# Attention and two MoE layers on one core: the head and the first pass put under the planner's due times, blocks 0 and 1 in feature halves, PSUM banks from one pool

## The chip, the core and the metric

One NeuronCore of a Trainium2 chip runs the whole program. The metric is the device time of one execution in microseconds (us); before the change the median of three runs is 935.18 us. Engines are named as in the profile: PE (TensorE matmul), PEld (its weight loads), DVE (VectorE), ACT (ScalarE), POOL (GpSimd), SP (the queue that issues nearly all DMAs). TensorE's clock has two levels, 1.2 and 2.4 GHz, and a granted clock of 1.00 is the upper one.

## The reference

Batch 4, 8 heads, 576 positions, head dimension 64; then two feed-forward layers over 2304 tokens, 512 wide, with 2048 features.

```python
# for every head: attention over q, k, v averaged in groups of 4, repeated 4 times,
# plus attention in a band |i - j| < 4; the two results are added
out_up    = np.repeat(sm_attn(mean4(q), mean4(k), mean4(v)), 4, axis=2)
out_local = softmax(where(band, scale * q @ k.T, -1e9)) @ v
x  = (out_up + out_local)                   # as 2304 x 512
h  = x @ w_in;   x = (h * sigmoid(h)) @ w_out                    # layer 1
h  = x @ w_in2;  y = where(h > 0, h, exp(min(h, 0)) - 1) @ w_out2  # layer 2
```

Everything is fp32. The layers' products are made from high and low parts (hi, and lo = x - hi, both fp32r), three matmuls for one product. The weights' 16 tensors of the first pass and all later ones are decoded from pairs of 32-bit words by ACT and DVE before they are split.

## The kernel before, in words

**Three parts.** The *head* is the attention of batch 0 (4 pairs of heads). The *first pass* is the first half of layer 1's features (8 of 16 feature tiles, f = 0 to 7) for 9 blocks of 256 tokens, with the attention of batches 1 to 3 (12 pairs) run between its matmuls. The *paired part* (`paired`, L847) is all the rest: three passes of three "duos" of 768 tokens each, layer 1's second half and both halves of layer 2.

**Attention of a pair** (`attention`, L278) is a generator that stops at every `yield`: transposes of q and k (L293), copies out of PSUM on ACT (L301, L303), pooling by 4 on DVE (L306), banded scores (L315), mask and maximum on DVE, subtraction and scaling on POOL (L330, L389), exponentials on ACT, transposes of the results (L409, L418), and the two products (L426, L438), joined into `x32` on DVE (L446). Rows arrive by `load_rows` and `load_windows` (L199, L237).

**A unit (n, f) of the first pass** is `g1` (L485: 12 matmuls of 128x256 into `ph`, then tanh on ACT, a product on DVE, `gh` on ACT, `gl` on POOL) and, LAG = 3 units later, `g2` (L527: 12 matmuls into two banks y0, y1, evicted after f = 7 and stored). `split_x` (L457) makes a block's hi on ACT (L468) and lo on DVE (L474).

**Weights of the first pass** pass through `decode_w` and `split_w` (L160, L174): two ACT operations, three on DVE, one more on ACT, one on POOL (L182); 16 tensors of 512 KB, loaded into a ring of three (`load_w`, L136).

**What sets the order in the head and the first pass** is written out by hand. The loads stand in a list (L1059 to L1070), and `attention(3)` issues the rows of the next pair (batch 1) in its middle (L345). `step` (L1127) takes turns among the live pairs; `small_first` (L1101) takes turns among weights, paced by EARLY_PACE and DECODE_PACE; `tick` (L1190), called after every third matmul, gives attention a step when a pace counted from deadlines says so. `warm` (L252) puts in matmuls on zeros at fixed places, 40 in all. PSUM is cut into four pools of two banks (L89 to L92): attention takes turns through fixed lists of them (`bank`, L263), `ph` has two banks, a decoding weight two.

**What sets the order in the paired part** is a planner: every operation of ACT, DVE and POOL is a `Job` (L575) with an engine, a cost, predecessors, and a due time. `pump` (L619) puts out those that can start by the planner's clock, earliest start first. Matmuls stand in program order there (L944, L1033, L1035), and `need` forces what they wait for.

Instructions of one engine run in the order in which the program put them out; the planner works when the program is built and not on the chip.

Of the kernel before, what the change touches and what calls it, by code (L numbers as in the profile page):

```python
# [22 lines left out]
def attention_moe_moe2_kernel(ctx, tc, q, k, v, wi1, wo1, wi2, wo2, out):  # L23
# [28 lines left out]
    STEPS = 19  # L52
    TICKS = 8
    DECODE_PACE = 1.5
    EARLY_PACE = 1.2
    N_EARLY = 13
    WARM, FILL = 9, (8, 4, 4, 4)
    GROUP = 3
# [14 lines left out]
    for i in range(NW):  # L73
        lo, hi = a0[i], a0[i + 1] - 1
        assert q0[i] <= lo and hi < q0[i] + WIN
        assert w0[i] <= max(lo - 3, 0) and min(hi + 3, S - 1) < w0[i] + WIN

# [10 lines left out]
    nat = attn_pools.enter_context(tc.tile_pool(name="nat", bufs=2, side="right"))  # L88
    att = attn_pools.enter_context(tc.tile_pool(name="att", bufs=2, side="right"))  # L89
# [6 lines left out]
    mask = cpool.tile([P, NW // 2, WIN], F32, name="mask")  # L96

    def constants():
        make_identity(nc, ident)
        tmp = gp.tile([P, NB], F32, tag="t", name="masktmp")[:, :4 * WIN].rearrange("p (n w) -> p n w", w=WIN)  # L100
# [13 lines left out]


# [3 lines left out]
    wf = {}  # L119
    wt = {}  # L120
    wz = []


# [4 lines left out]
    at = {"unit": 0, "load": 0, "decode": 0, "split": 0, "ahead": 2, "loads": 2 * FP}  # L128

    def load_next():  # L130

        if at["load"] < at["loads"]:
            load_w(at["load"])
            at["load"] += 1

    def load_w(i):  # L136
        layer, f, which = order[i]
        src = wsrc[layer][which].bitcast(I32)
        st = stage.tile([P, 2 * DM], I32, tag="ws", name="ws", bufs=3)
        if which == 0:  # L140
            nc.sync.dma_start(
                st.rearrange("p (c f) -> p c f", c=KC),
                src[:, f * 2 * P:(f + 1) * 2 * P].rearrange("(c p) f -> p c f", p=P),
            )
        else:
            nc.sync.dma_start(st, src[f * P:(f + 1) * P, :])
        wst[i] = st


    def magnitude(i):  # L150

        if i < len(order) and i not in wf:
            st = wst[i].rearrange("p (n w) -> p n w", w=2)
            t = ps_d.tile([P, DM], F32, tag="d", name="pw").bitcast(I32)
            nc.scalar.activation(t.bitcast(F32), st[:, :, 1].bitcast(F32), AF.Abs, scale=65536.0)

            nc.scalar.activation(st[:, :, 0].bitcast(U32), st[:, :, 0].bitcast(U32), AF.Copy, scale=2.0 ** -29, bias=2.0 ** -10 - 0.5)
            wf[i] = t

    def decode_w(i):  # L160
        magnitude(i)
        yield
        st = wst.pop(i).rearrange("p (n w) -> p n w", w=2)
        t = wf[i]
        tf = t.bitcast(F32)
        nc.vector.tensor_scalar(tf, tf, 2.0, W_MAX, op0=ALU.max, op1=ALU.min)
        nc.vector.scalar_tensor_tensor(t, t, 3, st[:, :, 0], op0=ALU.logical_shift_left, op1=ALU.bitwise_or)
        yield
        wf[i] = stage.tile([P, DM], I32, tag="wf", name="wf", bufs=3)
        nc.vector.scalar_tensor_tensor(wf[i], st[:, :, 1], -(1 << 31), t, op0=ALU.bitwise_and, op1=ALU.bitwise_or)  # L170
        load_next()
        yield

    def split_w(i, engine):  # L174
        layer, f, which = order[i]
        src = wf.pop(i).bitcast(F32)
        hi = wpool.tile([P, DM], F32R, tag=f"wh{which}", name=f"wh{which}")
        lo = wpool.tile([P, DM], F32R, tag=f"wl{which}", name=f"wl{which}")
        wt[layer, f, which] = tuple(x.rearrange("p (c f) -> p c f", c=KC) if which == 0 else x for x in (hi, lo))
        nc.scalar.copy(hi, src)  # L180
        yield
        engine.tensor_tensor(lo, src, hi.bitcast(F32), ALU.subtract)  # L182
        yield


    x32 = xpool.tile([P, KC, NT], F32, name="x32")

    pairs = [(b, pr) for b in range(B) for pr in range(NPAIR)]
    loaded = {}
# [3 lines left out]
    borrowed = {}  # L193

    def borrow(i, name):
        at, n = {"qk": (S, 2 * S), "qkD": (3 * S, 2 * SD), "vd": (3 * S + 2 * SD, 2 * SD)}[name]
        return x32[:, pairs[i][1], at:at + n][:, :2 * 2 * D if name == "vd" else n]

    def load_rows(i, which, engine=None):  # L199
        b, h0 = pairs[i][0], 2 * pairs[i][1]  # L200
        src = (q, k, v)[which]
        if which == 2:

            if i < NPAIR:
                heads = [wpool.tile([P, DM], F32R, tag=tag, name="rows2").bitcast(F32) for tag in ("wh0", "wl0")]
            else:
                t = nat.tile([P, 4 * FAC * D], F32, tag="natv", name="rows2", bufs=1)
                heads = [t[:, :DM], t[:, DM:]]
            for j, t in enumerate(heads):
                (engine or nc.sync).dma_start(t[:HS], src[b, h0 + j].rearrange("(p r) d -> p (r d)", r=2 * FAC))  # L210
            loaded[i, which] = heads
            return

        if i in (1, 2):
            both = xs.tile([P, 2 * NB], F32R, tag=("xh", "xl")[which], name=f"rows{which}").bitcast(F32)
            ts = [both[:, :NB], both[:, NB:]]
            half = NTB // 2
            for j in range(2):
                for a in range(2):
                    (engine or nc.sync).dma_start(  # L220
                        ts[a][:TB, :half * 2 * D].rearrange("p (c e) -> p c e", c=half)[:, :, j * D:(j + 1) * D],
                        src[b, h0 + j].rearrange("(c p) d -> p c d", p=TB)[:, a * half:(a + 1) * half],
                    )
                borrowed[2 * i - 2 + which, j] = ts[j]
            loaded[i, which] = [t[:, c * 2 * D:(c + 1) * 2 * D] for t in ts for c in range(half)]
            return
        elif i == 3 and which == 0:
            borrowed["y"] = yp.tile([P, KC * NB], F32, tag="y", name="rows0")
            t = borrowed["y"]
        else:  # L230
            t = nat.tile([P, NTB * 2 * D], F32, tag="nat", name=f"rows{which}", bufs=2)
        t = t[:, :NTB * 2 * D].rearrange("p (c e) -> p c e", c=NTB)
        for j in range(2):
            (engine or nc.sync).dma_start(t[:TB, :, j * D:(j + 1) * D], src[b, h0 + j].rearrange("(c p) d -> p c d", p=TB))
        loaded[i, which] = [t[:, c] for c in range(NTB)]

    def load_windows(i):  # L237
        b, h0 = pairs[i][0], 2 * pairs[i][1]
        if i in (2, 3):
            vw = borrowed["y"][:, (i - 2) * NW * D:(i - 1) * NW * D].rearrange("p (n d) -> p n d", d=D)  # L240
        else:
            vw = nat.tile([P, NW, D], F32, tag="vw", name="vw")
        for j in range(2):
            rows = v[b, h0 + j]
            nc.sync.dma_start(
                vw[j * WIN:(j + 1) * WIN, :NW - 1, :],
                bass.AP(tensor=rows.tensor, offset=rows.offset, ap=[[D, WIN], [w0[1] * D, NW - 1], [1, D]]),
            )
            nc.sync.dma_start(vw[j * WIN:(j + 1) * WIN, NW - 1, :], rows[w0[-1]:w0[-1] + WIN, :])
        loaded[i, 3] = vw  # L250

    def warm(n):  # L252
        pz = ps_h.tile([P, 512], F32, tag="h", name="pz")
        for _ in range(n):
            nc.tensor.matmul(pz, wz[0][:, :P], wz[0][:, :512], start=True, stop=True)

    def load_pair(i):
        for which in range(3):
            load_rows(i, which)

    banks = [(ps_a, "a")]

    def bank(name):  # L263
        pool, tag = banks[0]
        banks.append(banks.pop(0))
        return pool.tile([P, 512], F32, tag=tag, name=name)

    ybanks = [(ps_y, "y0"), (ps_y, "y1")]

    def ybank(name):  # L270
        pool, tag = ybanks[0]
        ybanks.append(ybanks.pop(0))
        return pool.tile([P, 512], F32, tag=tag, name=name)

    def ring(name, n):
        return att.tile([P, NW * WIN], F32, tag="ring", name=name, bufs=5)[:, :n]

    def attention(i):  # L278
        b, pr = pairs[i]

        if i < NPAIR:
# [64 lines left out]
        if i >= 2:  # L346
            load_windows(i)
# [964 lines left out]
```

## Time and profile before

| | us |
|---|---|
| median of 3 runs (lowest, highest) | 935.18 (933.81, 935.58) |
| the profiled execution: its own time | 935.57 |
| its span, from the first to the last instruction | 933.8 |
| PE busy in it | 897.7 (96%) |
| DVE, ACT, POOL busy | 627.2, 537.1, 263.2 |
| DMA traffic | 101.27 MB, 108 GB/s over the span |

The span is 1.8 us shorter than the profiled execution's own time. Busy PE is not PE at its peak, since matmuls are pipelined and overlap in the trace: how fast they go is read from the distance of their starts. The slices of the page are 23.3 us wide.

### The profile page before, as it was taken

To read this page: it belongs to the slowest core of one execution; us is meant where nothing else is said; L and a number is where in the kernel's file an instruction comes from. 1 tells how busy PE (TensorE), PEld (TensorE's weight loads), DVE (VectorE), ACT (ScalarE), POOL (GpSimd) and SP (SyncE) were. 2 spreads that over 40 slices of the span, in tenths; PEclk is the share of its full clock that TensorE was granted. 3 is DMA by queue.
4 is the path that set the end of the run, shared out by engine and by line. 5 is a ranking of instruction groups with operands and counts; after the bars stand their busy time and mean duration, and the time that the engine had idled before them with its cause. 6 is when DMAs were issued, how large, how long until landed. Compare 5 with 4: busy or idle time off the path is not lost.

```text
span 933.8 us, 17299 instructions
## 1 busy us (share of the span) xinstructions
PE 897.7 (96%) x6656; PEld 830.8 (89%) x6661; DVE 627.2 (67%) x1132; ACT 537.1 (58%) x1247; POOL 263.2 (28%) x292
## 2 busy tenths in 40 slices
PE   8388999999999999999999999999999999999998
PEld 5267889998999898999999999889899898998996
DVE  6777554454445758895885987948849979375462
ACT  5676645544545556844825748648458586382550
POOL 3676554454452223231101322301013023000000
PEclk9679999999999999999999999999999999999999
DMA  9954443332339402623533225132321350230301
GB/s 186 204 174 106 98 101 80 95 82 65 92 105 316 158 24 80 214 68 125 170 126 95 74 102 170 54 105 91 114 83 52 136 180 35 68 102 34 102 1 68
DMA packets 106531, 101.27 MB, mean 108 GB/s; under 512 B 62544, under 2 KB 89168, under 8 KB 106448
## 3 DMA queue, kind: packets, MB, share of 16 engines
q1 hardware_dynamic: 104048, 99.57, 35.7%
q10 hardware_dynamic: 2400, 0.59, 0.4%
q8 instruction: 52, 0.85, 0.4%
q14 instruction: 31, 0.25, 0.1%
HBM read 76.55 MB, written 23.59 MB: 107 GB/s over the span
## 4 chain that ended last, share of the span: by engine, by line
PE 63%; DVE 2%; ACT 1%; issue 0%; ACTq 0%; DVEq 0%
PE pc L944 28%; PE pc L1035 21%; PE pc L1033 11%; PE y L542 2%; PE ph L498 1%; DVE t L516 0%; DVE raw L713 0%; DVE raw L767 0%; DVE part L997 0%; DVE raw L766 0%; DVE xlr L736 0%; DVE s1t L761 0%; DVE raw L717 0%; ACT t L513 0%; DVE wAA3l L736 0%
## 5 line engine op out<-in xcount | busy, mean ns | idle before, releaser
L522 POOL TENSOR_TENSOR gl<-t,gh 128x256 fp32r<-128x256 f32 x72 | 56.2, 782 | 130.2 <-ACT gh L519 122.1
L542 PE MATMUL y<-gh,wh 128*128 128x256 f32 x288 | 86.9, 302 | 0.0
L498 PE MATMUL ph<-xh,wh 128*128 128x256 f32 x288 | 77.9, 295 | 6.2 <-DVE t L516 5.1
L542 PE MATMUL y<-gh,wl 128*128 128x256 f32 x288 | 82.1, 285 | 0.0
L542 PE MATMUL y<-gl,wh 128*128 128x256 f32 x288 | 82.1, 285 | 0.0
L498 PE MATMUL ph<-xl,wh 128*128 128x256 f32 x288 | 76.2, 289 | 2.9 <-DVE xl L474 2.8
L516 DVE SCALAR_TENSOR_TENSOR t<-t,ph 128x256 f32<-128x256 f32 x72 | 30.0, 416 | 68.0 <-ACT t L513 67.9
L1035 PE MATMUL pc<-wl,grw 128*128 128x512 f32 x192 | 74.8, 389 | 0.0
L1035 PE MATMUL pc<-wh,glk 128*128 128x512 f32 x192 | 74.8, 389 | 0.0
L1035 PE MATMUL pc<-wh,ghk 128*128 128x512 f32 x192 | 74.7, 389 | 0.0
L1035 PE MATMUL pc<-wh,grw 128*128 128x512 f32 x192 | 74.7, 389 | 0.0
L944 PE MATMUL pc<-xhr,wSA 128*128 128x384 f32 x288 | 74.5, 334 | 0.0
L956 ACT COPY hg<-pc 128x384 f32<-128x384 f32 x54 | 25.9, 479 | 65.2 <-PE pc L944 64.3
L498 PEld LDWEIGHTS ph<-xh,wh 128*128 128x128 f32 x288 | 55.2, 192 | 8.6 <-DVE t L516 6.3
L498 PEld LDWEIGHTS ph<-xl,wh 128*128 128x128 f32 x288 | 55.2, 192 | 4.4 <-DVE xl L474 3.7
L542 PEld LDWEIGHTS y<-gh,wh 128*128 128x128 f32 x288 | 56.0, 194 | 2.2 <-issue 1.0
L519 ACT CAST gh<-t 128x256 fp32r<-128x256 f32 x72 | 29.3, 407 | 49.4 <-DVE t L516 49.3
L997 DVE SCALAR_TENSOR_TENSOR part<-pc,part 128x384 f32<-128x384 f32 (+1 forms) x42 | 24.8, 609 | 48.0 <-PE pc L1035 28.4
L542 PEld LDWEIGHTS y<-gl,wh 128*128 128x128 f32 x288 | 56.0, 194 | 0.0
L542 PEld LDWEIGHTS y<-gh,wl 128*128 128x128 f32 x288 | 55.8, 194 | 0.0
L513 ACT ACTIVATE t<-ph 128x256 f32<-128x256 f32 x72 | 27.4, 381 | 48.7 <-PE ph L498 42.6
L736 DVE TENSOR_TENSOR xlr<-xraw,xhr 128x768 fp32r<-128x768 f32 x47 | 46.3, 985 | 13.0 <-ACT xhr L733 12.9
(248 smaller groups left out, 2836.5 us busy)
## 6 DMA issues: line engine op xcount, KB each, us to landing
ws<-in_moe_w_in_dram SPq DMA_DIRECT2D x32, 512.0 KB
ws<-in_moe_w_out_dram SPq DMA_DIRECT2D x32, 512.0 KB
xraw<-x SPq DMA_DIRECT2D x24, 384.0 KB
rows<-in_v_dram SPq DMA_DIRECT2D x36, 144.0 KB
yp<-yo SPq DMA_DIRECT2D x9, 512.0 KB
xd<-x SPq DMA_DIRECT2D x4, 1152.0 KB
x<-part SPq DMA_DIRECT2D x6, 768.0 KB
yp<-yo SPq DMA_DIRECT2D x6, 768.0 KB
```

Source lines behind the costliest of these rows:

```text
L498: nc.tensor.matmul(ph[:, :nb], a[:, c, :], b[c], start=m == 0, stop=m == 3 * KC - 1)
L513: nc.scalar.activation(t, h, AF.Tanh, scale=0.5)
L516: nc.vector.scalar_tensor_tensor(t, t, 1.0, h, op0=ALU.add, op1=ALU.mult)
L519: nc.scalar.copy(gh, t)
L522: nc.gpsimd.tensor_tensor(gl, t, gh.bitcast(F32), ALU.subtract)
L542: nc.tensor.matmul(y[d // 2][:, h:h + nb], wm[:, sl], gm, start=f == 0 and m == 0 and d % 2 == 0, stop=f == FP - 1 and m == 2, skip_group_ ...
L736: other=("V", VEC_[width], lambda: nc.vector.tensor_tensor(lo(), src, hi().bitcast(F32), ALU.subtract)),
L944: nc.tensor.matmul(acc_, a[:, cs], b[:, c, :], start=fresh and c == 0 and m == 0, stop=c == 1 and m == 2, skip_group_check=True,)
L956: snap[after, j] = [Job("A", ACT_[NB], lambda dst=dst, acc_=acc_: nc.scalar.copy(dst, acc_), [], gate, due=soon)]
L997: nc.vector.scalar_tensor_tensor(dst, src, sc, dst, op0=ALU.mult, op1=ALU.add)
L1033: nc.tensor.matmul(y[d][:, :NB], wm[:, sl], gm, start=first, stop=last_)
L1035: nc.tensor.matmul(y[d], gm[:, sl], wm, start=first, stop=last_)
```

## The change

The planner is extended to the head and the first pass. PE and SP become engines of it ("P", "S"), loads are jobs with a modelled DMA time, and every transpose group, score group, g1 and g2 is a job with a due time. `pick` takes the job with the earliest start and, among those of its engine that start within 0.1 us, the one due first. So the generators, paces and hand-written lists go.

- `Slots` and `Hold`: a tile or bank is taken when the job that first writes it is put out, and comes free when its last user is. All eight PSUM banks are one such pool; a rule limits `ph` to 3, `ph` and y together to 6, and weight temporaries to 2. Only the first eight weights use a bank as temporary.
- Blocks 0 and 1 run as (0, f 0 to 3), (1, f 0 to 3), (0, f 4 to 7), (1, f 4 to 7), so that both blocks' y banks (four) are held at once; the other blocks are as before.
- Some operations choose their engine: copies out of PSUM ACT or DVE, attention's subtraction and scaling and pooled values POOL or DVE, x's lo POOL or DVE (it was DVE's), with a preference added (PREFER).
- In the head, until the first g1, `fill` puts a matmul on zeros (128x512) for every 0.22 us of a gap over 0.3 us that the planner sees on PE.
- Rows of batch 0 load whole (before, pairs 1 and 2 in halves); batch 1's loads take their place by due time. `keep_x` stores a batch of x by due time and not after all attention. The constant column for the sums is set three times in all and not once a pair.
- Units of block 0 with f < 3 are split in 8 and 4 matmuls, so that they can start before the weight's low part is there.
- In the paired part a weight's load is modelled by a DMA clock (1.9 + 1.75 + 1.0 us on an idle queue) where it was 7.1 us after the slot came free, the two ACT operations of a decode are two jobs, and the bank sets are those that come free first.

The number of matmuls on data is unchanged.

```diff
-    ps_y = ctx.enter_context(tc.tile_pool(name="ps_y", bufs=1, space=PSUM))
-    ps_h = ctx.enter_context(tc.tile_pool(name="ps_h", bufs=2, space=PSUM))
-    ps_a = ctx.enter_context(tc.tile_pool(name="ps_a", bufs=2, space=PSUM))
-    ps_d = ctx.enter_context(tc.tile_pool(name="ps_d", bufs=2, space=PSUM))
+    psum = ctx.enter_context(tc.tile_pool(name="psum", bufs=1, space=PSUM))
+    PREFER = {("G", "V"): 1.5, ("V", "G"): -1.5, ("A", "V"): 0.5, ("V", "A"): -0.5}
+    LATE, FRAC = 2.0, (0.5, 0.7, 0.85, 1.0)
+    SLACK, MOST_H, N_PSUM, SPLIT_F = 0.1, 3, 8, 3
+    T_MM, T_FIRST, T_PAIR = 0.1185, 44.0, 6.4
...
+    def bank_rule(held, kinds):
...
+        return h.get("h", 0) <= MOST_H and h.get("h", 0) + h.get("y", 0) <= 6 and h.get("w", 0) <= 2
...
+    def fill(t):
+        gap = t - clock_of["P"]
+        if banks.free:
+            filler(min(int((gap - 0.1) / 0.22), 40))
...
+            pj = Job(
+                "P", 0.085 * len(parts), flip, [lq] if n_ == 0 else [lk] if n_ == 1 else [lq, lk], lat=0.2,
...
+        psl = Job("P", 1.25, scores, copies, lat=0.2, takes=bank2 + [hE], uses=[hqk])
...
+        psd = Job("P", 0.5, pooled_scores, [red], lat=0.2, takes=bankd + [hED, hsm], uses=[hqkD])
...
+            pj = Job("P", 0.11 * (s1 - s0), flip, [norm], lat=0.2, takes=[bank] + ([haT] if s0 == 0 else []), uses=[hE])
...
+            pj = Job("P", 0.26, flip, [norm_d], lat=0.2, takes=[bank] + ([haD] if j == 0 else []), uses=[hED])
...
+        psu = Job("P", 0.5, out_d, flips_d + pv, lat=0.2, takes=[banku], uses=[hvd, haD])
...
+            pj = Job("P", 0.54, out_l, [lw] + flips[:1 + t], lat=0.2, takes=[bank], uses=[hw, haT])
...
+        for n in range(0, 2, 2):
+            for f0 in range(0, FP, FP // 2):
+                sequence += [(m, f) for m in (n, n + 1) for f in range(f0, f0 + FP // 2)]
+        sequence += [(n, f) for n in range(2, len(BLOCKS)) for f in range(FP)]
+        at_, t_ = {}, T_FIRST
...
+            t_ += 24 * T_MM + share.get(n, 0.0) * (1.0 if n > 1 else LATE if f >= FP // 2 else 2.0 - LATE)
...
+        run(g1_jobs[0, 0])
+        filling[0] = False
+        run([j for b_ in range(B) for j in batch_end[b_]] + [kept_x[b_] for b_ in range(B)] + [x for p_ in w_split.values() for x in p_])
```

## Rows read from the trace of the kernel before

**Rows 1.** The page, parts 1 and 2: busy time, and the granted clock in 40 slices.

```profile
PE 897.7 (96%) x6656; PEld 830.8 (89%) x6661; DVE 627.2 (67%) x1132; ACT 537.1 (58%) x1247; POOL 263.2 (28%) x292
...
PEclk9679999999999999999999999999999999999999
```

**Rows 2.** Five stretches: length, busy us (x instructions) by engine, clock, DMA share, GB/s.

```profile
0.00:63.40 63.40, 45.98 (x525) 30.59 (x530) 44.66 (x90) 41.58 (x112) 37.68 (x56) 0.78 0.85 191
63.40:84.00 20.60, 14.02 (x134) 12.54 (x132) 17.64 (x30) 14.27 (x31) 11.71 (x11) 0.92 0.47 131
84.00:147.70 63.70, 60.36 (x752) 54.41 (x747) 31.86 (x69) 35.03 (x118) 34.52 (x44) 0.97 0.40 96
147.70:375.00 227.30, 222.38 (x2324) 212.55 (x2323) 126.61 (x250) 117.50 (x329) 91.48 (x112) 0.99 0.37 110
375.00:930.70 555.70, 554.97 (x2934) 520.69 (x2932) 406.42 (x697) 328.74 (x661) 87.78 (x69) 1.00 0.30 98
```

**Rows 3.** The chain that ended last: start us, us, what.

```profile
322.99 1.44 PE y L542 x12
...
367.53 1.04 PE pc L944 x6
...
374.95 26.00 PE pc L944 x150
...
897.28 31.34 PE pc L1035 x138
```

**Rows 4.** PE's instructions in order of time: start us, us, what [idle before].

```profile
5.59 1.03 PE L293 MATMUL pst<-ident,rows 96*128 96x96 f32 x5 [0.25 <-DMA rows<-in_q_dram]
...
19.75 1.67 PE L255 MATMUL pz<-zeros 128*128 128x512 bf16 x7
...
63.37 0.38 PE L498 MATMUL ph<-xh,wh 128*128 128x256 f32 x1
...
78.52 0.86 PE L293 MATMUL pst<-ident,rows 96*128 96x96 f32 x5 [2.04 <-DVE wf L170]
...
80.45 0.41 PE L498 MATMUL ph<-xl,wh 128*128 128x256 f32 x1
80.67 0.41 PE L498 MATMUL ph<-xh,wh 128*128 128x256 f32 x1
...
150.77 0.28 PE L498 MATMUL ph<-xh,wh 128*128 128x256 f32 x1
```

**Rows 5.** 160 to 280 us as in rows 2; then PE's L498 alone; then L542 alone.

```profile
160.00:280.00 120.00, 119.08 (x1418) 111.70 (x1418) 55.25 (x120) 60.83 (x192) 56.45 (x72) 1.00 0.34 88
160.00:280.00 120.00, 48.33 (x334) 42.40 (x332) 1.00 0.34 88
160.00:280.00 120.00, 47.59 (x327) 41.76 (x327) 1.00 0.34 88
```

**Rows 6.** SP's queue in the head: start us, us, line, what it issues.

```profile
1.73 6.47 SPq L220 DMA_DIRECT2D rows<-in_q_dram  x8
...
34.52 0.34 SPq L146 DMA_DIRECT2D ws<-in_moe_w_out_dram  x1
34.91 1.26 SPq L234 DMA_DIRECT2D rows<-in_q_dram  x2
36.69 2.22 SPq L234 DMA_DIRECT2D rows<-in_k_dram  x2
38.95 2.83 SPq L210 DMA_DIRECT2D rows<-in_v_dram  x2
...
44.58 0.53 SPq L141 DMA_DIRECT2D ws<-in_moe_w_in_dram  x1
```

**Rows 7.** Two stretches of the head, columns as in rows 2.

```profile
24.00:48.00 24.00, 10.14 (x91) 6.97 (x94) 17.83 (x34) 16.03 (x45) 15.45 (x19) 0.65 1.00 216
48.00:63.40 15.40, 14.96 (x176) 10.88 (x175) 11.63 (x23) 13.62 (x30) 12.40 (x14) 0.67 0.50 164
```

**Rows 8.** DVE's line L474, its durations: ns shortest/median/longest, first and last start us.

```profile
L474 DVE TENSOR_TENSOR xl<-x,xh x36: 409/426/1348, 57.9 to 339.8; 128x256 fp32r<-128x256 f32 x36
```

More of the change, by code (lines that the diff above doesn't have):

```diff
@@ L186, in attention_moe_moe2_kernel @@
[L186 to L235, printed above, removed]
@@ L252, in warm @@
[L252 to L273, printed above, removed]
@@ new lines, in attention_moe_moe2_kernel, with __init__, can, give @@
+    filling = [True]
+    serial = [0]
+    class Slots:
+        def __init__(self, tiles, rule=None, takes=None, heirs=None):
+            self.free = [(0.0, n, t) for n, t in enumerate(tiles)]
+            self.rule, self.takes, self.heirs = rule, takes, heirs
+            self.held = {}
+            self.busy = {}
+        def can(self, kinds):
+            n = len(kinds)
+            if n > len(self.free) or self.rule is not None and not self.rule(self.held, kinds):
+                return None
+            return sorted(x[0] for x in self.free)[n - 1]
+        def give(self, entry):
+            if self.takes == 0:
+                self.heirs[entry[1]](entry)
+            else:
+                self.free.append(entry)
@@ new lines, in attention_moe_moe2_kernel, with __init__, take, done @@
+    class Hold:
+        def __init__(self, slots, kind=None):
+            self.slots, self.kind, self.tile, self.left, self.last, self.users = slots, kind, None, 0, 0.0, []
+        def take(self):
+            s_ = self.slots
+            self.slot = min(s_.free, key=lambda x: x[:2])
+            s_.free.remove(self.slot)
+            self.tile = self.slot[2]
+            s_.held[self.kind] = s_.held.get(self.kind, 0) + 1
+            s_.busy[self.slot[1]] = self
+            if s_.takes:
+                s_.takes -= 1
+                if s_.takes == 0:
+                    rest, s_.free = s_.free, []
+                    for entry in rest:
+                        s_.give(entry)
+        def done(self, job):
+            self.left -= 1
+            self.last = max(self.last, job.end)
+            if self.left == 0:
+                self.slots.held[self.kind] -= 1
+                del self.slots.busy[self.slot[1]]
+                self.slots.give((self.last, self.slot[1], self.tile))
@@ L583, in sooner, with after @@
+        def after(self, preds):
+            for p in preds:
+                self.preds.append(p)
+                if p.end is None:
+                    if not self.open_:
+                        cand.remove(self)
+                        blocked.add(self)
+                    self.open_ += 1
+                    p.after_me.append(self)
+                    p.sooner(self.due - self.dur - p.lat)
         def sooner(self, due):
@@ L611, in emit @@
             assert t is not None
-            waiting.remove(self)
+            cand.remove(self)
+            for h in self.takes:
+                h.take()
+            if self.eng == "P":
+                if filling[0]:
+                    fill(t)
+                now[0] = t + self.dur
             self.fn()
@@ L636, in need @@
                 need(job.preds)
+                while job.end is None and job.start() is None:
+                    pick().emit()
                 if job.end is None:
@@ new lines, in attention_moe_moe2_kernel, with filler @@
+    banks = Slots(bank_tiles, bank_rule)
+    def filler(n):
+        if n > 0:
+            entry = min(banks.free, key=lambda x: x[:2])
+            for _ in range(n):
+                nc.tensor.matmul(entry[2], wz[0][:, :P], wz[0][:, :512], start=True, stop=True)
+    def fill(t):
+        gap = t - clock_of["P"]
+        if banks.free:
+            filler(min(int((gap - 0.1) / 0.22), 40))
+    wz = []
+    wsrc = [(wi1, wo1), (wi2, wo2)]
+    wst = {}
+    wt = {}
+    GORD = [2 * j for j in range(FP // 2)] + [2 * j + 1 for j in range(FP // 2)]
@@ new lines, in attention_moe_moe2_kernel @@
+        weights_second(0, end_first, lambda k: "w2")
+        x_work(0, end_first, lambda k: "wide" if k < 1 else "ring" if k < 2 else "rest" if k == 2 else (0, k - 3, FP // 2 - 1))
+        last = len(BLOCKS) - 1
+        run([x_split[last, c] for c in range(KC)])
+        x_pools.close()
+        open_wide()
+        xring.append(ring_slot())
+        events["wide"] = now[0]
+        run([j for f in range(FP) for j in g1_jobs[last - 1, f]])
+        xring.append(ring_slot())
+        events["ring"] = now[0]
@@ new lines, in attention_moe_moe2_kernel @@
+        run([j for f in range(FP) for j in g1_jobs[last, f]])
+        open_rest()
+        events["rest"] = now[0]
+        base[0] = now[0] + 12 * T_MM
+        entries = [(a_, n_, t_, []) for a_, n_, t_ in banks.free] + [(1e6 + n_, n_, h_.tile, h_.users) for n_, h_ in banks.busy.items()]
+        entries.sort(key=lambda x: (any(h_ is banks.busy.get(x[1]) for h_ in acc[last]), x[0]))
+        half = len(entries) // 2
+        banksets.extend([[x[2] for x in entries[:half]], [x[2] for x in entries[half:]]])
@@ new lines, in attention_moe_moe2_kernel @@
+        ph1 = paired({e: [x[3] for x in entries[e * half:(e + 1) * half]] for e in range(2)})
+        rest = [j for f in range(FP) for j in g2_jobs[last, f] if j.end is None]
+        while rest:
+            next(ph1)
+            clock_of["P"] = now[0]
+            while rest and rest[0].open_ == 0 and (rest[0].end is not None or (rest[0].start() or 1e9) <= now[0] + 0.1):
+                if rest[0].end is None:
+                    rest[0].emit()
+                rest.pop(0)
+                pump(now[0])
```

1215 lines of the change are left out of this document (617 added, 598 removed).

## The prediction

> **What bounds the kernel now.** I read the page's busy time and clock first, then the busy time by stretches, then the chain that ended last, and PE's and SP's instructions in order of time where the first two show a loss. PE is busy for 96% of the span, and its granted clock is clearly down only in slices 2 and 3 [rows 1]. The stretches divide the kernel in two [rows 2]. From 375 us to the end PE is busy for 554.97 of 555.70 us, and the chain is matmul upon matmul there, from 374.95 us to the last step at 897.28 [rows 3]. Nothing that reorders other engines can shorten this; it can only break it. So everything that can be won lies before 375 us.
>
> The first g1 starts at 63.37 us [rows 4]. From there to 374.95 are 311.6 us. PE's work in them: a group of 12 matmuls takes 1.44 us back to back [rows 3], and 72 units have two groups each, 144 x 1.44 = 207.4 us. For attention I take 160 to 280 us, where PE is busy for 119.08 us and the clock is 1.00: 334 + 327 = 661 matmuls belong to units (x 0.12 = 79.3 us), the other 757 take 39.8 us, and a pair has 121 of them, so a pair costs PE 6.36 us [rows 5]; 12 pairs are 76.3 us. Three groups of the paired part at 1.04 us are mixed into the end [rows 3]: 3.1 us. Together 286.8 us, so 311.6 - 286.8 = 24.8 us are lost. Of that PE is idle for 6.58 + 3.34 + 4.92 = 14.8 us (length less busy time in stretches two to four [rows 2]); the rest is the lower clock and changes between kinds of matmul.
>
> The head is the other loss: 63.4 us for four pairs, which cost PE 4 x 6.36 = 25.4 us at full clock. What limits it? DMA at first: share 1.00 and 216 GB/s from 24 to 48 us [rows 7]. Batch 0's rows are 4 x (6 x 144 + 320) KB = 4.85 MB (shapes of the reference, windows with their overlap), 22.5 us at that rate, but the weights and, from 34.91 to 41.8 us, the rows of batch 1 go in between: no weight load is issued between 34.52 and 44.58 [rows 6]. Of ACT, DVE and POOL none is full: in those 24 us they are busy for 16.03 + 17.83 + 15.45 = 49.3 us, 2.05 engines of three; the densest stretch, 48 to 63.4, has 37.65 / 15.4 = 2.44 [rows 7]. The order costs the rest.
>
> **The change part by part.**
>
> *Head.* By 63.4 us the three engines have done 44.66 + 41.58 + 37.68 = 123.9 us of work [rows 2], with 13 weights begun. The first g1 needs one, and four are needed within the next few units. A weight costs the three engines 5.3 us by the planner's own costs (0.62 + 0.66 + 0.62, 0.70 + 0.69 + 0.69, 1.30), so nine that wait are 47.5 us: 76.4 us remain. Data come at 5.59 us [rows 4]. At 2.05 engines busy that is 5.6 + 37.3 = 42.9 us, at 2.44 it is 36.9. *Fill* adds to it: the planner prices a pair's PE work at 1.02 + 1.25 + 0.5 + 0.55 + 0.52 + 0.5 + 1.08 = 5.42 us where the rows give 6.36, and packs every gap that it sees with matmuls of 0.22 us, which is what they take (seven in 1.67 us [rows 4]). So PE has no slack to catch up: 4 x 0.94 = 3.8 us late. Sum: 46.7 us; I take **48 us** for the first g1. Ends: 41 (denser) and 60 (weights still go first). Fewer, whole loads take six DMAs of 6.47 / 8 = 0.81 us off SP's queue, and batch 1's rows, 1.26 + 2.22 + 2.83 us of issue [rows 6], go behind the weights; both lie inside these 48 us. Next to be late are batch 1's rows; their attention is due only after the first units.
>
> *First pass.* The 286.8 us of PE work stay. Feature halves ask for four features' weights in the first eight units, so the PE idle of the second stretch (6.58 us [rows 2]; 2.04 of it in one wait at 78.52 behind a weight's DVE work [rows 4]) should go in part, but more work now runs in less time. By 147.7 us the engines have done 94.2 (DVE), 90.9 (ACT) and 83.9 (POOL), 269 us in all [rows 2]; block 2 follows at 150.77 [rows 4]. For PE alone block 2 could start at 48 + 29 x 1.44 + 25.4 = 115 us (16 g1, 13 g2, four pairs). At 2.44 engines the other work takes until 5.6 + 110.2 = 116 us, at 2.05 until 137. So PE and the others bind nearly together. **Lost: 15 us** (ends 5 and 30), about what the old order loses after 84 us (24.8 less the second stretch's idle and its clock of 0.92), with some 9 of it before block 2, which then starts near 124.
>
> *PSUM.* While blocks 0 and 1 hold four y banks, ph takes up to two, and attention and weight temporaries share the rest; before, attention had four banks to take turns in. No row prices this wait: nothing at best, and the delay of the third rival at worst; I put it inside the 15.
>
> *x's lo* leaves DVE for POOL in most cases: 36 instructions of 0.43 us off DVE [rows 8], 0.74 on POOL by the planner's cost, beside matmuls; at nothing, since POOL is busy for 91 of 227 us in the fourth stretch [rows 2]. The same instruction has taken 1348 ns against a median of 426 [rows 8]. The Trainium skill's page "SBUF — State Buffer" (section "Who interferes with whom") says that a VectorE instruction with two SBUF inputs and a GpSimd instruction that reads SBUF exclude each other for a whole instruction. The spread in that row agrees; by the rule, what moves to POOL still blocks DVE now and then, by up to the 0.9 us of the row, and the sum would be a few us more where DVE is on the path.
>
> *Paired part.* Same matmuls, same order; 555.7 us stay. Its cover is DVE at 406 of 556 us and ACT at 329 [rows 2]. The shorter modelled load lets ACT queue for a load earlier than it lands; tanh and evictions stand behind it. At nothing, with 0 and +8 as ends: PE can't gain, and a us or so at each of a few stage changes is what idle engine time would not cover. The constant column and the stores of x lie beside other work.
>
> *Sum.* 48 + 286.8 + 15 = 349.8 us instead of 374.95, so 25.2 us less. The profiled execution took 935.57 us (span 933.8), 0.4 above the median of 935.18. 935.57 - 25.2 = **910 us**. A difference under 0.2% (1.9 us) can't be told from none.
>
> **Rivals.** *A, forecast:* 900 to 919 us, chance 0.50.
>
> *B, only PE binds:* at 2.44 engines busy and with 3.8 us of lag g1 starts at 41, and 8 us are lost: 335.8, 39 us less, 896 us. For it: that density was reached in 48 to 63.4 [rows 7]. Against it: never longer than 15 us. 0.15.
>
> *C, the other engines or the banks bind until block 2:* block 2 starts at 137 (2.05 engines busy). From block 2 to 374.95 the old order takes 374.95 - 150.77 = 224.2 us: 361.2, 14 us less, 922 us. For it: that rate is what the head had from 24 to 48. 0.15.
>
> *D, slower: PE's clock falls.* After the last filler PE meets weights and x that are just in time. After the wait of 2.04 us at 78.52 matmuls start 0.22 us apart at 80.45 and 80.67 [rows 4] where 0.12 is full pace; in 24 to 63.4 the granted clock is 0.65 and 0.67 [rows 7]. PE's work in blocks 0 and 1 is 29 x 1.44 + 25.4 = 67.2 us; at the lower level it grows by 0.10 / 0.12, 56 us at most. The gain of 25 is gone when 45% of it runs so; with three fifths it is +34 - 25 = 9 us, 944 us. Against it: from 84 us on, with waits of under 1 us, the clock was 0.97 and more [rows 2]. 0.15. The Trainium skill's page "TensorE: Matmul & The Clock Gate" (section "HAM oscillation — how this bites in real kernels") describes this loss: short bursts of matmuls between waits, each begun at the lower clock. The row at 80.45 agrees for one wait.
>
> *E, it does not do what it says:* DMA holds the head whatever the order, g1 starts above 60, and 25 us are lost as before: 933 to 937 us. Against it: the weights' gap of 10 us [rows 6]. 0.05.
>
> **Numbers.** A, B and C are faster: 0.80; E 0.05; D 0.15. The range takes in A, B and C with their bounds and leaves out D and E: 893 to 932.
>
> **What would show it.** First g1 at 45 to 51 us, more matmuls on zeros in the head and its clock near 1.00; block 2's first g1 near 124; the last unit's g2 near 350; the paired part 556 us long. Wrong, if PE's idle time from the first g1 to block 2 is above 20 us, if the clock there is under 0.9, or if the paired part grows by more than 2 us.

## The result and the profile after

The changed kernel takes **909.81 us** (905.92 to 911.03, four executions) against 935.38 beside it: ratio 0.9715, 95% interval [0.9675, 0.9755]. The forecast was 910 us, and faster. The profiled execution is the fastest of the four, 905.92 us (span 904.1), so the trace has to explain 935.57 - 905.92 = 29.65 us. Between the medians there are 25.57 us, 4 less: the profiled execution of the changed kernel is that much below its median.

The page after, parts 1 and 2, to set beside [rows 1]:

```profile
PE 885.2 (98%) x6673; PEld 823.2 (91%) x6673; DVE 630.5 (70%) x1145; ACT 538.0 (60%) x1221; POOL 274.9 (30%) x304
...
PEclk9899999999999999999999999999999999999999
```

Busy time by stretches after (columns as in [rows 2]); 54.11 us is the first g1:

```profile
0.00:54.11 54.11, 46.69 (x613) 31.53 (x613) 34.38 (x76) 29.15 (x88) 34.08 (x59) 0.91 0.90 192
54.11:75.00 20.89, 18.81 (x144) 17.50 (x144) 19.60 (x37) 18.07 (x46) 18.88 (x19) 1.00 0.86 242
75.00:104.00 29.00, 25.56 (x313) 23.62 (x313) 27.06 (x42) 19.54 (x50) 20.07 (x21) 1.00 0.57 148
104.00:137.00 33.00, 31.49 (x423) 28.32 (x420) 22.01 (x43) 22.35 (x71) 28.37 (x35) 0.95 0.36 92
137.00:345.20 208.20, 208.00 (x2259) 201.85 (x2258) 117.48 (x254) 113.30 (x310) 82.57 (x101) 1.00 0.39 111
...
346.90:900.60 553.70, 552.96 (x2923) 518.68 (x2921) 409.25 (x697) 333.92 (x658) 90.89 (x73) 1.00 0.30 99
```

The chain that ended last, after (columns as in [rows 3]):

```profile
345.15 1.04 PE b L1185 x6
...
346.91 23.93 PE b L1185 x138
...
867.17 31.34 PE b L1275 x138
```

The last step begins at 867.17 where it began at 897.28 [rows 3]: 30.11 us earlier (0.4 of them come back behind it, to the end of the span). The paired part's first long step begins elsewhere (138 matmuls here, 150 there), but its end can be compared: 346.91 + 23.93 = 370.84 where it was 374.95 + 26.00 = 400.95, also 30.11 us earlier. So the paired part kept its length, and the point that stood at 374.95 is now 374.95 - 30.11 = 344.84.

**Where the 30 us came from.** Block 2's first g1 starts at 136.58 where it started at 150.77 [rows 4]: 14.2 us.

```profile
136.58 0.36 PE L845 MATMUL b<-xh,wh 128*128 128x256 f32 x1
```

The other 15.9 us lie behind it: 344.84 - 136.58 = 208.3 us instead of 224.2. There PE is now busy for 208.00 of 208.20 us, where it idled 4.92 of 227.30 [rows 2]: 4.7 us. Less was also left to do: at block 2 all 192 matmuls of g2 of blocks 0 and 1 are done, against 156 recorded before (36 x 0.12 = 4.3 us), while attention stands at the same point in both. The rest, some 7 us, is closer packing of the units' matmuls: behind block 2, g1's 672 are busy for 90.08 us where they took 95.74, and g2's 668 recorded ones for 90.22 where 710 took 100.27.

**What the head does.** SP's queue after (columns as in [rows 6]), then PE's instructions (as in [rows 4]):

```profile
26.78 0.43 SPq L344 DMA_DIRECT2D ws<-in_moe_w_in_dram  x1
27.32 1.04 SPq L488 DMA_DIRECT2D nat<-in_q_dram  x2
28.46 3.08 SPq L488 DMA_DIRECT2D nat<-in_k_dram  x2
31.58 1.12 SPq L492 DMA_DIRECT2D natv<-in_v_dram  x2
...
46.02 0.35 SPq L349 DMA_DIRECT2D ws<-in_moe_w_out_dram  x1
```

```profile
34.00 0.60 PE L527 MATMUL b<-ident,nat 96*128 96x96 f32 x5 [1.52 <-DMA nat<-in_q_dram]
...
37.07 1.35 PE L527 MATMUL b<-ident,nat 96*128 96x96 f32 x7 [1.16 <-DMA nat<-in_k_dram]
...
38.21 1.49 PE L320 MATMUL b<-t 128*128 128x512 bf16 x3
39.49 1.17 PE L705 MATMUL b<-ident,ring 72*72 72x72 f32 x8
40.59 1.35 PE L570 MATMUL b<-qk 64*64 64x64 f32 x40
...
54.11 0.47 PE L845 MATMUL b<-xh,wh 128*128 128x256 f32 x1
```

`nat` and `natv` are batch 1's rows here. They are issued before the fourth weight, and their transposes (L527) stand in PE's queue ahead of the pooled transposes (L705) of a pair of batch 0, waiting for DMA while everything behind them waits too: ACT is idle for 5.33 us before 40.22, POOL for 2.77 before 37.65.

```profile
40.22 0.87 ACT L715 COPY ring<-b 72x288 f32<-72x288 f32 x2 [5.33 <-PE b L705]
```

```profile
37.65 0.72 POOL L662 TENSOR_TENSOR natv<-natv 72x256 f32<-72x256 f32 x1 [2.77 <-DMA natv<-in_v_dram]
```

### The profile page after: what moved, and what is told of

Its sections match the earlier page's. It is cut to its first block, busy times and chain, and to the rows that moved or that the text cites. A ratio compares the mean times of both kernels' runs of the same rounds, so it can differ in the third digit from the quotient of the medians.

```text
span 904.1 us, 17255 instructions
## 1 busy us (share of the span) xinstructions
PE 885.2 (98%) x6673; PEld 823.2 (91%) x6673; DVE 630.5 (70%) x1145; ACT 538.0 (60%) x1221; POOL 274.9 (30%) x304
## 4 chain that ended last, share of the span: by engine, by line
PE 86%; DVE 3%; POOL 2%; DMA 1%; issue 1%; ACT 0%; DVEq 0%; SPq 0%; POOLq 0%; ACTq 0%
PE b L1185 29%; PE b L1275 22%; PE b L1273 11%; PE b L883 9%; PE b L845 9%; PE b L750 2%; DMA ws<-in_moe_w_out_dram 1%; PE b L527 1%; PE b L727 1%; PE b L683 1%; PE b L705 1%; PE b L622 1%; PE b L570 0%; DVE wf L383 0%; POOL xl L796 0%
## 5 line engine op out<-in xcount | busy, mean ns | idle before, releaser
L883 PE MATMUL b<-gh,wh 128*128 128x256 f32 x288 | 84.7, 294 | 0.0
L883 PE MATMUL b<-gl,wh 128*128 128x256 f32 x288 | 81.9, 284 | 0.0
L883 PE MATMUL b<-gh,wl 128*128 128x256 f32 x288 | 81.8, 284 | 0.0
L845 PE MATMUL b<-xh,wh 128*128 128x256 f32 x288 | 74.4, 291 | 0.4 <-DVE t L866 0.4
L1275 PE MATMUL b<-wl,grw 128*128 128x512 f32 x192 | 74.8, 389 | 0.0
L1275 PE MATMUL b<-wh,glk 128*128 128x512 f32 x192 | 74.8, 389 | 0.0
L1275 PE MATMUL b<-wh,ghk 128*128 128x512 f32 x192 | 74.7, 389 | 0.0
L1275 PE MATMUL b<-wh,grw 128*128 128x512 f32 x192 | 74.7, 389 | 0.0
L1185 PE MATMUL b<-xhr,wSA 128*128 128x384 f32 x288 | 74.5, 334 | 0.0
L845 PE MATMUL b<-xl,wh 128*128 128x256 f32 x288 | 72.3, 283 | 0.7 <-POOL xl L796 0.7
```

The source lines that it names most:

```text
L845: nc.tensor.matmul(ph.tile[:, :NB0], w[a][:, c, :], x_slot(n, c, b_), start=start and m == 0, stop=stop and m == len(products) - 1,)
L883: nc.tensor.matmul(y[d // 2].tile[:, o:o + NB0], w[m // 2][:, sl], gg(m % 2), start=f == 0 and m == 0 and d % 2 == 0, stop=fin and m == 2, ...
L1185: nc.tensor.matmul(acc_, a[:, cs], b[:, c, :], start=fresh and c == 0 and m == 0, stop=c == 1 and m == 2, skip_group_check=True,)
L1275: nc.tensor.matmul(y[d], gm[:, sl], wm, start=first, stop=last_)
```

## The experiments

Twelve kernels, in three groups; those of a group ran on one chip beside the kernel before (936.76, 936.08 and 935.33 us). "Idle" is PE's from the first g1 to 137 us; "other work" is the busy time of DVE, ACT and POOL up to 137 us (before: 91.23 + 84.55 + 79.07 = 254.9); "last step" is the start of the last 138 matmuls in the chain. Differences below are of medians; where two kernels are of different groups, the ratios give the same to about 1 us.

| kernel | median us | ratio, interval | first g1 | idle | other work | last step |
|---|---|---|---|---|---|---|
| the change again | 906.36 | 0.9679 [0.9656, 0.9702] | 52.7 | 6.6 | 292.4 | 867.2 |
| no halves | 910.22 | 0.9721 [0.9699, 0.9743] | 53.6 | 8.5 | 282.9 | 870.9 |
| no matmuls on zeros | 904.70 | 0.9664 [0.9639, 0.9689] | 50.7 | 6.4 | 294.2 | 865.9 |
| held | 903.79 | 0.9650 [0.9629, 0.9670] | 49.0 | 5.9 | 297.0 | 864.8 |
| held, no zeros | 908.74 | 0.9705 [0.9678, 0.9733] | 49.4 | 6.9 | 289.5 | 867.6 |
| held, true prices | 910.83 | 0.9731 [0.9711, 0.9751] | 49.2 | 7.6 | 292.8 | 870.0 |
| held, loads too | 907.06 | 0.9690 [0.9677, 0.9703] | 48.0 | 9.0 | 296.6 | 868.7 |
| before, rows later | 941.09 | 1.0059 [1.0045, 1.0073] | 64.1 | | 249.8 | 899.6 |
| x's lo on DVE | 915.06 | 0.9777 [0.9755, 0.9798] | 61.9 | 6.1 | 278.9 | 873.8 |
| held, no halves | 915.36 | 0.9780 [0.9760, 0.9801] | 49.2 | 11.5 | 280.7 | 876.8 |
| true prices | 906.40 | 0.9690 [0.9668, 0.9712] | 59.7 | 4.3 | 289.0 | 869.4 |
| held, weights sooner | 903.30 | 0.9654 [0.9633, 0.9675] | 52.0 | 5.0 | 297.3 | 865.0 |

**1. The change again.** No edit.

> The changed kernel once more, as the measure for the runs beside it. 906 to 911 us, first g1 near 54 us, paired part 553.7 us as in its first profile. If the 4 us between its executions are TensorE's clock, a profile at a lower mean clock than 0.992 shows a stretch of the first pass or head at the lower level and is longer by about that much.

It repeats: 906.36 us. Two profiles of one kernel put the first g1 at 54.1 and 52.7 us with the same last step (867.17 and 867.22), the scale for what follows.

**2. Blocks one after the other** (no feature halves).

```diff
-        for n in range(0, 2, 2):
-            for f0 in range(0, FP, FP // 2):
-                sequence += [(m, f) for m in (n, n + 1) for f in range(f0, f0 + FP // 2)]
-        sequence += [(n, f) for n in range(2, len(BLOCKS)) for f in range(FP)]
+        sequence += [(n, f) for n in range(len(BLOCKS)) for f in range(FP)]
```

> Blocks 0 and 1 feature by feature, block after block, all else as in the changed kernel. Theory (the halves let the first eight units run on four features' weights): PE idle between the first g1 and block 2 grows from 7 us to 12 or more, the time by 4 to 8 us. Rival (the due-time order brings the gain, the halves nothing): within 2 us of the changed kernel. A new plan shifts every operation, so under 2 us says nothing.

3.9 us slower; the last step is 3.6 us later, 2.0 of it idle time of PE before 137 us. That is the low end of the theory's time, without its 12 us of idle time.

**3. No matmuls on zeros** between the head's real ones.

```diff
-    filling = [True]
+    filling = [False]
```

> No matmuls on zeros in gaps of the head (the first nine stay). Theory of the prediction (they pack PE and cost 3.8 us of lag): first g1 2 to 4 us earlier, at 50 to 52. Rival (they hold the clock up): clock in the head falls from 0.91 to 0.7 or less, PE's work there (25 us at full clock) grows, first g1 at 55 us or later, the time 1 to 6 us longer.

904.70, the intervals overlap: here they buy nothing. The granted clock up to the first g1 is 0.82 instead of 0.97 (0.91 in the first profile), and the first g1 is 2 us sooner all the same (50.7, as the theory had it). The planner's clock doesn't count the zeros, so the order of the rest is the change's.

**4. Batch 1 held.** Transposes and pooled values of batches 1 to 3 are planned only after batch 0's last pooled transposes; loads stay free.

```diff
-        prior = []
+        prior = list(head_gate) if b >= 1 else []
...
-            pv.append(alike(1.2, halves, 0.68, whole, [lv], main="G", takes=[hvd] if j == 0 else [], uses=[hv]))
+            pv.append(alike(1.2, halves, 0.68, whole, [lv] + (head_gate if b >= 1 else []), main="G", takes=[hvd] if j == 0 else [], uses=[hv]))
...
+        if i == NPAIR - 1:
+            head_gate.extend(flips_d)
```

> In the plan, transposes and pooled values of batches 1 to 3 come after the pooled transposes of batch 0's last pair; loads stay. Theory (batch 1's operations stand in PE's and POOL's queues before the last pair's, wait for their DMA, and hold the head): PE's and ACT's waits of 32 to 40 us go, first g1 at 48 to 50 instead of 54.1; 3.9 us of PE work moves behind it, so the time falls by 0 to 3 us. Rival (DMA or the engines' work hold the head): first g1 at 53 or later and the time 2 to 5 us longer, since that work is now behind.

903.79 us, and the first g1 at 49.0. The stretch from 24 to 48 us (columns as in [rows 2]), first in the change again, then held:

```profile
24.00:48.00 24.00, 19.17 (x307) 14.41 (x304) 17.61 (x38) 15.07 (x46) 15.99 (x20) 0.93 0.80 201
```

```profile
24.00:48.00 24.00, 23.61 (x319) 15.70 (x315) 17.76 (x40) 19.42 (x56) 18.62 (x22) 1.00 0.77 194
```

The three engines do 55.8 us of work instead of 48.7 in the same time, and PE stands still for 0.4 us instead of 4.8. So batch 1 in the head's queues was what made the first g1 late: it lies at 48.0 to 49.4 us in the held plans of 4 to 7 and 10, and at 50.7 or later in every plan that is not held. No execution of this kernel (903.38 to 904.40) is as slow as one of the change on the same chip (904.85 to 907.87). The next wait, held:

```profile
54.72 0.58 PE L848 MATMUL b<-xh,wh 128*128 128x256 f32 x1 [2.56 <-ACT wh L825]
55.10 0.41 PE L848 MATMUL b<-xl,wh 128*128 128x256 f32 x1
55.31 0.41 PE L848 MATMUL b<-xh,wh 128*128 128x256 f32 x1
```

From 54.70 to 56.50 us the granted clock is 0.50.

**5. Held, and no zeros** (edits 4 and 3).

> Batch 1's operations held as in e5 and no fillers. e5 began g1 at 49.0 us with 581 matmuls in the head and a clock of 1.00. Theory (fillers cost about 2 us, as e2's first g1 at 50.7 against 52.7 to 54.1 says): first g1 at 46.5 to 48, 901 to 903 us. Rival (with the wait for batch 1 gone, the fillers fit and keep the clock): first g1 at 49 or later, 904 to 908.

The first g1 stays (49.4), as the rival had it; the time is 5 us more, in executions from 904.14 to 911.74. The order of work is that of 4, so here the zeros are worth some us: the clock from 24 to 48 us is 0.79 without them and 1.00 with them.

**6. Held, with PE's attention priced as the trace has it.**

```diff
-        psd = Job("P", 0.5, pooled_scores, [red], lat=0.2, takes=bankd + [hED, hsm], uses=[hqkD])
+        psd = Job("P", 0.83, pooled_scores, [red], lat=0.2, takes=bankd + [hED, hsm], uses=[hqkD])
```

and so psu 0.5 to 0.84, local output 0.54 to 0.91, psD's transposes 0.26 to 0.31, scores 1.25 to 0.94.

> Batch 1's operations held, and the five PE costs of the planner set to what the trace shows (0.94, 0.83, 0.31, 0.84, 0.91 us). Theory (the planner's prices are what makes fillers late): first g1 at 46 to 48, fewer fillers, 901 to 903 us. Rival (prices don't matter where PE waits for others): first g1 within 1 us of 49, time within 2 us of e5's 903.8.

The first g1 does not move (49.2), and the whole is 7 us slower, which neither had: another plan, with 1.7 us more idle time of PE up to 137 us and 2.7 us of waits of PE behind DVE (`hgw`, `hg`) in the paired part. So an edit of a few prices can cost 7 us here; a smaller difference between two plans says little of the edited part by itself.

**7. Held, loads too.**

```diff
+        if b >= 1:
+            for j_ in (lq, lk, lv):
+                j_.after(head_gate)
```

> The loads of q, k and v rows of batches 1 to 3 come, in the plan, after batch 0's last pooled transposes (and so all that hangs on them); weights have the DMA engines to themselves meanwhile. Theory (what costs is batch 1 in the head, operations and loads): first g1 at 47 to 49 as in e5, the weights' tensors 4 to 8 earlier by some us, but batch 1's attention later; 900 to 906 us. Rival (batch 1 needs its rows early): PE idle before block 2 over 12 us, 908 to 914.

The earliest first g1, 48.0, with PE at clock 1.00 throughout to 137 us, and yet 3.3 us slower than 4: PE idles 9.0 us up to 137 us, and 5.1 of them are waits for batch 1's `qk` and rings, which are then late.

**8. The kernel before, batch 1's first rows loaded after the head.**

```diff
-        if NPAIR - 1 <= i < len(pairs) - 1:
+        if NPAIR <= i < len(pairs) - 1:
...
         for _ in first_x:
             pass
+        load_pair(NPAIR)
```

> The kernel BEFORE, with batch 1's first rows loaded after the head and not in its middle; nothing else. Theory of the prediction (the 10 us without a weight load are part of what the old order costs): first g1 3 to 6 us earlier than 63.4, 930 to 934 us. Rival (the old head is held by its turns and not by DMA): first g1 within 1 us of 63.4, and the first pass up to 6 us longer because the rows come late: 935 to 942.

5 us slower than before, first g1 at 64.1. With the rows gone from the head, the old one is no shorter. One weight's load goes out sooner, at 39.34 and not at 44.58, the next does not (45.46 after 45.21; SP's queue here, then in the kernel before):

```profile
39.34 0.39 SPq L141 DMA_DIRECT2D ws<-in_moe_w_in_dram  x1
45.46 0.33 SPq L146 DMA_DIRECT2D ws<-in_moe_w_out_dram  x1
```

```profile
45.21 0.45 SPq L146 DMA_DIRECT2D ws<-in_moe_w_out_dram  x1
```

So the 10-us gap between weight loads did not hold the old head; that its own turns did is what is left, and not shown.

**9. x's lo on VectorE again.**

```diff
-                "G", GPS_[NB0],
-                lambda n=n, c=c, src=src: nc.gpsimd.tensor_tensor(...), [a],
-                other=("V", VEC_[NB0], lambda n=n, c=c, src=src: nc.vector.tensor_tensor(...)),
+                "V", VEC_[NB0],
+                lambda n=n, c=c, src=src: nc.vector.tensor_tensor(...), [a],
```

> The change, with the lower half of x taken off POOL again: all of these subtractions on VectorE, as before the change. It tests the prediction's step that the move costs and brings nothing (36 instructions of about 0.43 us on an engine that is not full). Theory A (the step holds): within 3 us of the changed kernel on the same chip, about 903 to 910 us, PE's idle time from the first g1 to 137 us at 6 to 10 us, the paired part 553 to 556 us long. Theory B (the move is part of the gain): 36 x 0.43 = 15 us more on VectorE before the paired part hold up g2 or x, 912 us or more, with more idle time of PE behind VectorE. Theory C (the two engines exclude each other, so that the move costs): 902 us or less.

8.7 us slower: theory B's time, and the largest loss from any single edit to the change. Theory B's other sign, more idle time of PE, did not come (6.1 us); the first g1 comes at 61.9. The subtraction's durations (ns shortest/median/longest), in the change and on VectorE:

```profile
L796 POOL TENSOR_TENSOR xl<-x,xh x31: 721/731/742, 31.8 to 268.0; 128x256 fp32r<-128x256 f32 x31
```

```profile
L796 DVE TENSOR_TENSOR xl<-x,xh x36: 410/426/3189, 35.4 to 300.8; 128x256 fp32r<-128x256 f32 x36
```

The longest stands against three of POOL's instructions that follow each other (VectorE and POOL in order of time, same kernel):

```profile
103.82 3.19 DVE L796 TENSOR_TENSOR xl<-x,xh 128x256 fp32r<-128x256 f32 x1
```

```profile
103.67 1.14 POOL L651 TENSOR_TENSOR ring<-ring,sm 72x576 f32<-72x576 f32 x1 [0.45 <-DVE sm L648]
104.77 0.74 POOL L868 TENSOR_TENSOR gl<-t,gh 128x256 fp32r<-128x256 f32 x1
105.47 1.26 POOL L825 TENSOR_TENSOR wl<-wf,wh 128x512 fp32r<-128x512 f32 x1
```

It ends at 107.01, 0.3 us after the third ends (106.73). POOL's instructions are lengthened too, if not this one: in the change, a subtraction of the same shape took up to 1240 ns.

```profile
L869 POOL TENSOR_TENSOR gl<-t,gh x48: 722/734/1240, 59.7 to 265.9; 128x256 fp32r<-128x256 f32 x48
```

The 1240 ns begin 0.04 us after a VectorE instruction on two SBUF tensors:

```profile
106.39 0.68 DVE L383 SCALAR_TENSOR_TENSOR wf<-ws,wf 128x512 int32<-128x512 int32 x1
```

```profile
106.43 1.24 POOL L869 TENSOR_TENSOR gl<-t,gh 128x256 fp32r<-128x256 f32 x1
```

**10. Held, no halves** (edits 4 and 2).

> The held version (transposes and pooled values of batches 1 to 3 planned after batch 0's last pooled transposes) without feature halves. Theory A (the halves are worth what their removal from the changed kernel cost, 3.9 us, because four features' weights are asked for in eight units instead of eight): 3 to 5 us above the held version, 906.5 to 909 us, and PE idle 3 us longer in the 30 us after the first g1, behind weights. Theory B (the 3.9 us were the reshuffle of the plan that any edit brings, as with true prices): within 2.5 us of the held version either way, 901.5 to 906 us, or a loss that lies somewhere else than behind weights in those 30 us.

11.6 us slower than held, far more than either theory had. From 75 to 104 us:

```profile
75.00:104.00 29.00, 23.57 (x204) 20.64 (x203) 27.33 (x40) 19.47 (x47) 20.19 (x18) 0.73 0.56 145
```

PE has 204 matmuls where 4 has 333, idles 5.4 us there and 6.0 before it, and the granted clock is 0.73. Of its waits some are for weights, as theory A wanted (2.0 us for `wl`, 1.1 more), more are for attention's rings (2.1, 1.2, 1.2 and less).

**11. True prices, nothing held** (edit 6 alone).

> The change with PE's attention prices set to the durations of the trace (pooled scores 0.83 for 0.5, pooled output 0.84 for 0.5, local output 0.91 for 0.54, flips 0.31 for 0.26, scores 0.94 for 1.25), nothing held. Theory A (the prediction's term: matmuls on zeros packed too tightly put the first g1 3.8 us late): first g1 at 49 to 50.5 us instead of 52.7 to 54.1, time 902 to 904 us. Theory B (the head is late because of batch 1's operations in its queues, whatever the prices): first g1 at 52 to 55 us, time 904 to 910 us as the rest of the plan falls out.

Theory B, and more: the first g1 at 59.7. The head's end there:

```profile
56.71 3.57 PE L320 MATMUL b<-t 128*128 128x512 bf16 x8 [4.70 <-ACT qk L551]
59.72 0.78 PE L845 MATMUL b<-xh,wh 128*128 128x256 f32 x1
```

PE waits 4.70 us, before eight matmuls on zeros, for a bank that ACT empties of batch 1's transposes. Yet the time is that of the change (906.40): the 77.3 us from there to 137 hold only 4.3 us of idle time, and 73.0 us of PE's work where the change has 77.8 behind its head. So most of what the head lost was work done early.

**12. Held, first six weights due 6 us sooner.**

```diff
-            prepare(i, dues[pos] - 1.0 if which == 0 else dues[pos + LAG] - 1.0)
+            prepare(i, (dues[pos] if which == 0 else dues[pos + LAG]) - (7.0 if i < 6 else 1.0))
```

> The held version with the due times of the first six weights 6 us earlier, so that their loads and their work on ScalarE, VectorE and POOL go ahead of part of batch 0's last pair. Theory A (behind the held version's first g1 at 49 us the first units wait for weights, 2.56 us of PE at 54.7 us, and the head has slack for them): first g1 at 48 to 50 us, PE's idle time from it to 137 us at 2 to 4 us instead of 5.9, 900 to 902.5 us. Theory B (the head's queues are full, so what goes ahead puts the last pair back by as much): first g1 at 51 to 54 us, the wait gone all the same, 903 to 907 us.

903.30, no different from 4. As theory B had it, the wait for the weight is gone, PE is busy from the first g1 to 75 us without a gap, and the first g1 is 3 us later. These two are the fastest seen, 0.965 of the kernel before against 0.968 for the change (intervals that overlap a little).

What the due times, PSUM's common pool, the choice of engines for attention's operations and the split units are each worth was not tried; it stays open.

## Why the prediction was right, and where it was not

The total was right through errors that cancel. The sum was 48 + 286.8 + 15 = 349.8; the trace has 54.1 for the first g1. Of the 286.8 us of PE work, 72 matmuls of batch 1 (24 transposes, 40 of `qk`, 8 of `qkD`) were done before it, 72 x 39.8 / 757 = 3.8 us, so 283.0 lay behind. The stretch is 344.84 - 54.11 = 290.7, so 7.7 us were lost. Against the forecast: +6.1 - 3.8 - 7.3 = -5.0 us. The median lies 3.9 above the profiled execution, and so at 910: that part is luck. Of the signs that were named, the first g1 (45 to 51) and block 2 (near 124) failed; the last g2 (ends at 346.91, for 350), more matmuls on zeros in the head (56, from 40) and the paired part's length came; the head's clock, near 1.00, came in the second profile (0.97) rather than the first (0.91).

*First g1 at 48:* late by 6.1 us (4.7 in the second profile). The rate was met, the amount was not. DVE, ACT and POOL did 34.38 + 29.15 + 34.08 = 97.6 us of work in 54.1 - 5.6 us, 2.01 engines where 2.05 was taken; the step had 76.4 us. Three of its terms were mis-sized. Weights: the seven groups of the old head come to 52.5 us, not 13 x 5.3 = 68.9, since ACT had begun 11 and POOL had 9; so the rest of the head's work was 123.9 - 52.5 = 71.4, not 55. Their rows in the kernel before, up to 63.4 us (groups by line):

```profile
L157 ACT ACTIVATE ws<-ws 128x512 uint32<-128x512 uint32 x11 | 7.3, 661 | 0.0
...
L180 ACT CAST wh<-wf 128x512 fp32r<-128x512 f32 x10 | 6.2, 619 | 0.0
...
L166 DVE TENSOR_SCALAR pw<-pw 128x512 f32<-128x512 f32 x10 | 6.9, 694 | 6.5 <-ACT pw L155 6.5
...
L182 POOL TENSOR_TENSOR wl<-wf,wh 128x512 fp32r<-128x512 f32 x9 | 11.3, 1270 | 1.1 <-ACT wh L180 1.1
```

(with L155 7.0, L167 7.0, L170 6.8). Weights in the new head: 12.7 us of such work by 54.1 us, so they were put off further than the four assumed (21.2). And batch 1, assumed behind, came in with 8.8 us, its values and reductions first. Together 92.9 of the 97.6 us; the other 4.7 were not traced. The largest piece of batch 1 (after, to 54.1 us):

```profile
L662 POOL TENSOR_TENSOR natv<-natv 72x256 f32<-72x256 f32 x4 | 2.9, 722 | 3.2 <-DMA natv<-in_v_dram 3.2
```

That batch 1's rows "go behind the weights" was the step that failed: they go ahead of the fourth weight. Held, the head does as much (97.3 us) by 48.95, at 2.24 engines, so without batch 1's waits the rate rises too.

*Filler lag, 3.8 us:* shown in part, and not for the reason given. In the change's own order the first g1 is 2.0 to 3.4 us sooner without zeros (50.7 for 52.7 and 54.1). But held it is at 49.0, 49.4 without zeros and 49.2 with true prices: neither the zeros nor the price of a pair delays it there.

*Lost 15 us:* 7.7, and not where I had them. From the first g1 to block 2 are 136.58 - 54.11 = 82.5 us, and PE's work there, at the sum's prices, is 32 groups and 484 matmuls of attention, 32 x 1.44 + 484 x 39.8 / 757 = 71.5 us. So 10.9 us were lost there (7.0 of them idle time of PE, 2.08 + 3.44 + 1.51), where I put some 9. Behind it the 208.3 us hold 0.20 of idle time and are 3.2 less than the sum's 283.0 - 71.5 = 211.5: where I put 6 us of loss, the price of the work was too high.

*Block 2 near 124:* 136.6, since the first g1 came 6.1 us later, three more groups of g2 (4.3 us) were done before it, and 1.9 us more were lost. That is rival C's mark (137), by chance: C had 269 us of the other engines' work by then at 2.05 engines, and there were 293.6 us (before, to 137 us: 254.9) at 2.23. All idle time of PE there is in waits for those engines, the longest of them these (waited for: us in all, times, longest):

```profile
PE b L705 <- DVE ring L582: 2.5, 1, 2.5
PE b L845 <- POOL wl L826: 1.4, 2, 1.0
PE b L705 <- POOL ring L651: 1.2, 1, 1.2
```

That they bind all the way to block 2 is not shown. And C went on with the old 224.2 us behind block 2, which became 208.3.

*Feature halves:* right in sign, no term of their own; worth 3.9 us in the change and 11.6 in the held plan. By experiment 6 a plan's own scatter is up to 7 us, so the first figure alone would show nothing; the second is beyond it.

*x's lo at nothing:* the kernel with the subtraction back on VectorE is 8.7 us slower. I divided POOL's load by a stretch where it has room (91 of 227 us), and left out that VectorE has little before block 2 (27.06 of 29.00 us from 75 to 104). How much of the 8.7 is the subtraction and how much the plan that came out with it is not separated; it is little more than the 7 us of experiment 6. The rule of the Trainium skill's page "SBUF — State Buffer" (section "Who interferes with whom"), that a VectorE instruction with two SBUF inputs contends with a GpSimd instruction that reads SBUF, was worked out as a cost of the move. The rows of experiment 9 agree with the rule, with a loser on either side (3189 ns on VectorE, 1240 on POOL); the instruction moved keeps to 721 to 742 ns on POOL.

*Paired part at nothing:* right. From the end of its first long step to the start of the last it takes 496.33 us in both (897.28 - 400.95, 867.17 - 370.84).

*Rival D, PE's clock:* not in this kernel, 0.95 to 1.00 after the first g1 (at least 0.93 in the stretches of the second profile). It is real all the same: 0.73 in experiment 10, and 0.50, the lower level of 1.2 GHz, after the 2.56-us wait of experiment 4, where matmuls start 0.21 us apart and not 0.12. Its evidence against, "waits of under 1 us" from 84 us on, was misread; the kernel before has a longer one there, at a clock of 0.97 for the stretch:

```profile
127.81 0.63 PE L293 MATMUL pst<-ident,rows 96*128 96x96 f32 x5 [1.39 <-ACT qk L301]
```

*Rival B:* its loss of 8 us is what came (7.7), its first g1 at 41 is not. *Rival E:* the head did shorten. *Its evidence, the weights' gap:* fell with experiment 8.

## What to carry to other kernels

In a plan with in-order queues, look at the next stage's work that a due time lets in early: one transpose waiting for its rows holds a whole queue. Delaying such work brought the first g1 from 52.7 to 49.0 us; the plan with it was 2.6 us faster, less than what a replan alone can move. The start of the first useful matmul is a poor target by itself (49 to 60 us at nearly the same total); count what all engines have done by the point from which PE never waits. And when a scheduler replans everything after each edit, measure how far an indifferent edit moves the time before a part is given a price (here the same five prices cost 7 us in the held plan and nothing in the change).

## What was not expected of the hardware

VectorE's subtraction of two SBUF tensors can lose to three POOL instructions in a row (3.19 us for 0.43), and a subtraction on POOL to one of VectorE's (1.24 us for 0.73).

PE's granted clock was low also where no single wait was long: from 75 to 104 us of experiment 10 the longest was 2.15 us, and it was 0.73. In the change's own head, waits of 1.52 and 1.16 us go with 0.79 from 24 to 48 us in the first profile, one of 2.79 us with 0.93 in the second, and the held plan, with 0.4 us of idle time there, has 1.00. What decides between these is not shown. Executions of the change without any edit run from 904.85 to 911.03 us, and in the first four the mean clock goes with it (0.992 at the fastest, 0.984 at the slowest).
